# A quarter of q in fp32 by SyncE, z ahead of kv in the opening, and a reordered batch 1 and chunk 1

## The chip, the cores and the metric

The kernel runs on one core of a Trainium2 chip. The metric is the device time of one execution in microseconds (us). The core has a matmul engine (TensorE, PE; PEld is its weight load), a vector engine (VectorE, DVE), a scalar engine for pointwise functions (ScalarE, ACT), a general engine (GpSimd, POOL) and a sequencer without arithmetic (SyncE, SP). SP, ACT and POOL can issue transfers (DMAs). An engine executes its own instructions in program order; between engines the order comes from semaphores. Matmul results land in PSUM, eight banks of 512 fp32 columns on 128 partitions; everything else lies in SBUF.

## The reference

The inputs are q, k and v, each (8 batches, 8 heads, 576 positions, 64), and two weights, w_in (512 x 2048) and w_out (2048 x 512), all fp32.

```
def phi(x):
    return np.where(x > 0, x, np.exp(x) - 1.0) + 1.0
q_p, k_p = (phi(q), phi(k))
kv = np.einsum('bhsd,bhse->bhde', k_p, v)
z = np.sum(k_p, axis=2)
num = np.einsum('bhsd,bhde->bhse', q_p, kv)
den = np.einsum('bhsd,bhd->bhs', q_p, z)[..., None] + 1e-06
x = (num / den), heads side by side: 4608 rows of 512
h = x @ w_in
out = (h - np.tanh(h)) @ w_out
```

phi is computed as min(exp(x), max(x, 0) + 1), with an exp on ScalarE, a maximum with an addition on VectorE (`r`), and a minimum on VectorE.

## The kernel before

**Two stages.** The attention works batch by batch (576 rows each) and writes xT, the normalised result transposed to 512 x 4608 in bf16. The two dense layers work in nine chunks of 512 rows. Layer 1 of a chunk computes 16 groups `fi` of 128 hidden columns (four 512-column matmuls each, L366), two groups at a time go through tanh (L372, in chunk 0 one at a time, L377) and a subtraction into gT (L373, L378). Layer 2 runs in 16 steps `s` of four matmuls (L387); a finished row block is copied out of PSUM by ScalarE (`evac`, L396) and stored by two transfers of SP (L401). In chunk 0 layer 2 is cut the other way round: step s works with the weights of quarter `s // 4` on row block `s % 4`, so that it starts with a quarter of w_out, and all four evacuations come in steps 12 to 15. Layer 1 and the later chunks' layer 2 rotate over PSUM banks 0 to 5; attention work uses banks 6 and 7, in chunk 0 banks 4 to 7 (`side`).

**Order by hand.** The program order is the schedule. The lists `s1[fi]` and `s2[s]` hold attention work that is issued after group fi of layer 1 and after step s of layer 2. In chunk c the work of batch c + 1 (`n1`) is finished and that of batch c + 2 (`n2`) is begun. The work of a batch is: load q, k, v (POOL transfers that cast fp32 to bf16; a tile holds rows in two halves i, each half in two parts h), phi of k and q (`a_kphi`, `a_qphi`, L134 to L136), the transposes of q (`a_qT_pe` on TensorE, L164 with copies at L168 and L170, or a transposing transfer of SP, `a_qT_dma`, L153), kv and z by matmuls over the positions with a mask product into kz (`a_kv`, L177 and L186; or `a_kv_cols`, L199 and L202, which reads a copy `vp` of v with a column of ones behind it, made by `a_vp`, L189), the denominators (`a_den`, L276, L281, reciprocal L285), and the numerators. The reciprocals reach all partitions through DRAM (`a_spread`: four stores of SP into ds, L305, two broadcast loads into rdb, L308; `a_num` then multiplies, L317 and L328), or, for batches 0 and 1, by a matmul with a selection matrix (`b0_spread`, L240; `a_spread_pe`, L354, after `a_split`, L295 to L298, has cut the reciprocal into bf16 parts), with the numerators copied to `ns` by ScalarE first (L233; L344 and L346) and multiplied at L244 and L359.

**The loads.** POOL issues, in this order: q(0) in two halves, k(0) in two halves, the identity matrix, v(0) in two halves, w_in in ten parts, k(1), two quarters of w_out, q(1), some memsets, v(1), two quarters of w_out. Eight of POOL's transfers can be out at once: the ninth waits for the first, and so on. From chunk 1 on, POOL waits at `gate` (L383) for the transposed q of batch c + 1 before it issues the loads of batch c + 2.

**The opening.** Up to the first dense layer the order is: phi of q(0), half by half; 18 matmuls on zeros (`spin`, L444); transposes of half 0; phi of k(0) half 0, exp of k(0) half 1 in two parts; five spins; transposes of half 1; a selection matrix built on ScalarE (L460, L462); six spins; z of half 0 (`b0_z`, L210); the minima of k half 1; z's mask product (`b0_zc`, L214); kv of half 0 (`b0_kv`, L221) and its mask product (`b0_kz`, L225); z of half 1 and its mask product; the denominators of batch 0; numerators, kv of half 1, spread and scaling (L231 to L244). `b0_scale_rest` (L263) finishes the last 64 rows of batch 0 in chunk 0.

**Chunk 0 and chunk 1.** In chunk 0, `s2[7]` holds both halves of the transposes of q(1) and then kv of batch 1, `s2[8]` the rest of batch 0, `s2[9]` the denominators of batch 1, `s2[10]` its numerators and the split, `s2[11]` and `s2[13]` the two halves of the spreading; phi of q(2) lies in `s2[12]` to `s2[14]` (the last with the transposing transfer), phi of k(2) half 0 in `s2[15]`. In chunk 1, `s1[1]` has phi of k(2) half 1, `s1[3]` the two copies of v(2), `s1[7]` kv of batch 2 and `s1[10]` its denominators and their spreading; its numerators are in `s2[11]` to `s2[15]`. From chunk 2 on kv is in `s1[5]` and the denominators in `s1[8]`.

The tile gT has one buffer, so each chunk's gT waits until the one before is read.

Of the kernel before, what the change touches and what calls it, by code (L numbers as in the profile page):

```python
# [18 lines left out]
def kernel(  # L19
# [9 lines left out]
    nc = tc.nc  # L29
# [55 lines left out]
    def load(b, t, src, halves):  # L85

        x = src[b].rearrange("h (p j) d -> (h p) (j d)", j=J)
        if halves:
            for i in range(2):
                nc.gpsimd.dma_start(out=t[:, :, i].rearrange("q h j d -> q h (j d)"),  # L90
                                    in_=x.rearrange("(h i q) x -> i q h x", h=2, i=2)[i])
        else:
            nc.gpsimd.dma_start(out=t.rearrange("q h i j d -> q (h i) (j d)"),
                                in_=x.rearrange("(n q) x -> q n x", n=4))
# [26 lines left out]
    def phi_pieces(b, src, store, name, i, parts=0):  # L121

        if i == 0:
            store[b] = work.tile([128, 2, J, 2, D], BF16, name=name)
        x = src[b][:, :, i]
        e = epool.tile([128, 2, J, D], BF16, name="e")
        r = epool.tile([128, 2, J, D], BF16, name="r")
        y = store[b][:, i].rearrange("p j h d -> p h j d")
        if parts:

            return ([lambda h=h: nc.scalar.activation(e[:, h], x[:, h], AF.Exp) for h in range(2)],
                    lambda: nc.vector.tensor_scalar(r, x, 0.0, 1.0, ALU.max, ALU.add),
                    [lambda h=h: nc.vector.tensor_tensor(y[:, h], e[:, h], r[:, h], ALU.min) for h in range(2)])
        return (lambda: nc.scalar.activation(e, x, AF.Exp),  # L134
                lambda: nc.vector.tensor_scalar(r, x, 0.0, 1.0, ALU.max, ALU.add),  # L135
                lambda: nc.vector.tensor_tensor(y, e, r, ALU.min))  # L136
# [54 lines left out]
    def a_kv_cols(b, banks):  # L191
        kp = kp_t[b]
        kz_t[b] = kz_c[b % 2]
        ps = [banks()[:, 0:272].rearrange("p (i e) -> p i e", i=2) for hg in range(2)]
        for i in range(2):
            for j in range(J):
                for hg in range(2):
                    r = slice(64 * hg, 64 * hg + 64)
                    nc.tensor.matmul(ps[hg][:, i, :], kp[r, i, j].rearrange("p h d -> p (h d)"),  # L199
                                     vp[r, i, j, :], start=(j == 0), stop=(j == J - 1))  # L200
        for hg in range(2):
# [205 lines left out]
    nc.scalar.activation(act0, zero[:, 0:1], AF.Exp)  # L407
    load_q(0)
# [44 lines left out]
    (ek0, rk0, mk0), (ek1, rk1, mk1) = (phi_pieces(0, k_t, kp_t, "kp", i, 2 * i) for i in range(2))  # L453
    for f in (ek0, rk0, *ek1, mk0, rk1):
        f()
# [46 lines left out]
    for c in range(NC):  # L502
# [4 lines left out]
        if c == 0:  # L507
# [35 lines left out]
            s2[12].append(lambda: q2(0))  # L543
            s2[13].append(lambda: (spread1(1), q2(1)))
            s2[14].append(lambda: q2(2))
            s2[15].append(lambda: a_kphi(2, 0))
        elif n1 < B:
            s1[7 if c == 1 else 5].append(lambda: a_kv_cols(n1, attn))
            s1[10 if c == 1 else 8].append(lambda: (a_den(n1, attn), a_spread(n1)))
            for p in range(NP + 1):  # L550
                s2[(11 if c == 1 else 9) + p].append(lambda p=p: a_num(n1, p))
        if c == 1:
            s1[1].append(lambda: a_kphi(2, 1))
            for i in range(2):
                s1[3].append(lambda i=i: a_vp(2, i))
# [87 lines left out]
```

## Time and profile before

| | value |
|---|---|
| runs | median 295.15 us of 4 (294.8 to 295.48) |
| profiled execution | 295.1 us, of which the span from the first to the last instruction is 293.3 |
| granted TensorE clock | 0.998 |
| first exp of q(0) (L134) | 5.70 us |
| reciprocal of batch 0 (L285) | 13.71 to 14.77 us |
| steady L366 from | 17.77 us |
| layer 2 of chunk 0 (L387) from | 31.16 us |
| layer 1 of chunk 1 (L366) from | 51.22 us |
| layer 1 of chunk 2 (L366) from | 82.34 us |
| end of the last L387 group on the chain of waits | 279.18 us |
| q0, POOL's transfers | 18.35 MB in 17,552 packets |
| q1, transfers of SP | 20.17 MB in 21,344 packets |

A profile row gives start and duration in us, engine and line, the operation with output<-input, the shape and how many instructions are merged; a bracket holds the idle time in front of it and what ended it. Lines are those of the kernel before. A matmul's duration is longer than the distance to the next one, because matmuls are pipelined. Durations of a transfer are either the issuing time on its queue (rows of SPq and POOL) or the time to landing, where the row says so. Idle time of an engine that is not on the path to the end costs nothing by itself.

### The profile page before, as it was taken

The page shows a single profiled execution, that of the slowest core. Times are in us where ns is not written, and L with a number is a line of the kernel's source. Part 1 is how long each engine was busy: PE and PEld are TensorE (multiplying, and loading weights), DVE is VectorE, ACT ScalarE, POOL GpSimd, SP SyncE. Part 2 cuts the span into 40 slices and gives each one's busy share as a digit, 9 for nine tenths or more (in the row PEclk, how much of TensorE's full clock was granted, in tenths as well). Part 3 has the DMA queues.
Part 4 walks back from the last instruction along what each step waited for, and adds up shares of the span by engine and source line. Part 5 has one row for each costly group of instructions (what it writes and reads, how often), then busy time and mean ns, then how long its engine had stood idle before and what let it go on. Part 6 is the DMA issues. An engine that isn't in the chain of part 4 may idle for free.

```text
span 293.3 us, 4475 instructions
## 1 busy us (share of the span) xinstructions
PE 283.7 (97%) x1772; PEld 134.3 (46%) x1801; DVE 174.7 (60%) x265; ACT 139.5 (48%) x168; POOL 33.5 (11%) x55
## 2 busy tenths in 40 slices
PE   8899998999999999999999999999999999999994
PEld 2544453354444444544454445444444444444443
DVE  4759957887467764786478646865581456106600
ACT  3938537947334653455246524661452155126411
POOL 8673030030030003000300020000000000000000
PEclk9999999999999999999999999999999999999999
DMA  7999999987999658955895669577117310131032
GB/s 99 194 204 213 208 206 217 205 141 139 239 161 194 153 122 139 220 126 117 137 223 127 141 134 179 114 176 146 38 25 176 73 36 0 38 81 27 0 74 72
DMA packets 39077, 38.94 MB, mean 133 GB/s; under 512 B 16336, under 2 KB 33808, under 8 KB 38288
## 3 DMA queue, kind: packets, MB, share of 16 engines
q0 software_dynamic: 17552, 18.35, 38.8%
q1 hardware_dynamic: 21344, 20.17, 30.1%
q8 instruction: 14, 0.23, 0.3%
q10 hardware_dynamic: 160, 0.13, 0.1%
q14 instruction: 7, 0.06, 0.1%
HBM read 43.91 MB, written 9.55 MB: 182 GB/s over the span
## 4 chain that ended last, share of the span: by engine, by line
PE 69%; DMA 17%; issue 7%; POOL 2%; DVE 1%; ACT 1%; SPq 1%; POOLq 0%; DVEq 0%
PE ps_all L366 34%; PE ps_all L387 30%; DMA qraw<-in_q_dram 6%; DMA w_in_sb<-in_moe_w_in_dram 3%; DMA rdb<-ds 3%; PE ps_all L199 2%; DMA out_dram<-osb 2%; DMA kraw<-in_k_dram 2%; PE ps_all L317 2%; DMA ds<-rden 1%; PE ps_all L276 1%; ACT osb L396 1%; SPq L401 0%; POOL qraw L90 0%; ACT e L134 0%
## 5 line engine op out<-in xcount | busy, mean ns | idle before, releaser
L366 PE MATMUL ps_all<-xT,w_in_sb 128*128 128x512 bf16 x560 | 127.0, 379 | 1.1 <-DVE xT L244 0.3
L387 PE MATMUL ps_all<-w_out_sb,gT 128*128 128x512 bf16 x547 | 126.3, 379 | 0.7
L373 DVE TENSOR_TENSOR gT<-ps_all,th 128x1024 bf16<-128x1024 f32 x64 | 77.9, 1218 | 59.8 <-ACT th L372 59.8
L372 ACT ACTIVATE th<-ps_all 128x1024 f32<-128x1024 f32 x64 | 65.5, 1024 | 57.0 <-PE ps_all L366 46.4
L366 PEld LDWEIGHTS <-w_in_sb 128*128 128x128 bf16 x576 | 55.2, 98 | 66.6 <-issue 0.6
L387 PEld LDWEIGHTS <-gT 128*128 128x128 bf16 x560 | 54.1, 98 | 64.5 <-issue 0.6
L396 ACT COPY osb<-ps_all 128x512 f32<-128x512 f32 (+1 forms) x36 | 20.9, 582 | 73.7 <-PE ps_all L387 57.4
L328 DVE TENSOR_TENSOR xT<-ps_all,rdb 128x512 bf16<-128x512 f32 x24 | 16.3, 689 | 13.7 <-PE ps_all L317 11.2
L134 ACT ACTIVATE e<-qraw 128x1152 bf16<-128x1152 bf16 x16 | 18.5, 1161 | 7.0 <-DMA qraw<-in_q_dram 7.0
L134 ACT ACTIVATE e<-kraw 128x1152 bf16<-128x1152 bf16 x15 | 17.5, 1165 | 0.1
L136 DVE TENSOR_TENSOR qp<-e,r 128x1152 bf16<-128x1152 bf16 x16 | 12.0, 757 | 8.0 <-ACT e L134 7.4
L136 DVE TENSOR_TENSOR kp<-e,r 128x1152 bf16<-128x1152 bf16 x15 | 11.4, 758 | 8.1 <-ACT e L134 7.3
L383 POOL COPY g<-qT 1x1 bf16<-1x1 bf16 x5 | 1.1, 226 | 120.9 <-DMA qT<-qp 120.9
L378 DVE TENSOR_TENSOR gT<-ps_all,th 128x512 bf16<-128x512 f32 x16 | 10.3, 685 | 2.4 <-ACT th L377 1.7
L377 ACT ACTIVATE th<-ps_all 128x512 f32<-128x512 f32 x16 | 9.2, 598 | 4.3 <-PE ps_all L366 3.1
L317 PE MATMUL ps_all<-qT,kz 128*128 128x512 bf16 x28 | 10.1, 379 | 0.2 <-DVE xT L328 0.2
L444 PE MATMUL ps_all<-zero 128*128 128x512 bf16 x29 | 8.8, 464 | 1.2 <-DVE zero L405 1.2
L135 DVE TENSOR_SCALAR r<-qraw 128x1152 bf16<-128x1152 bf16 x16 | 7.3, 454 | 2.2 <-DMA qraw<-in_q_dram 2.2
L199 PE MATMUL ps_all<-vp,kp 64*128 64x136 bf16 x216 | 7.4, 220 | 0.4 <-POOL g L383 0.4
L199 PEld LDWEIGHTS <-kp 64*128 64x128 bf16 x216 | 6.4, 94 | 3.0 <-issue 2.1
L285 DVE RECIPROCAL rden<-den 128x144 f32<-128x144 f32 x7 | 7.4, 1053 | 0.2
L394 DVE COPY osb<-ps_all 128x128 f32<-128x128 f32 x1 | 0.3, 291 | 11.6 <-DMA out_dram<-osb 11.6
(82 smaller groups left out, 121.8 us busy)
## 6 DMA issues: line engine op xcount, KB each, us to landing
out_dram<-osb SPq DMA_DIRECT2D x70, 128.0 KB
rdb<-ds SPq DMA_DIRECT2D x12, 576.0 KB
kraw<-in_k_dram POOLq DMA_DIRECT2D x7, 576.0 KB, 7.4
qraw<-in_q_dram POOLq DMA_DIRECT2D x7, 576.0 KB, 9.0
v<-in_v_dram POOLq DMA_DIRECT2D x7, 576.0 KB, 11.9
w_out_sb<-in_moe_w_out_dram POOLq DMA_DIRECT2D x4, 512.0 KB, 16.2
w_in_sb<-in_moe_w_in_dram POOLq DMA_DIRECT2D x6, 256.0 KB, 8.7
qraw<-in_q_dram POOLq DMA_DIRECT2D x2, 288.0 KB, 4.8
```

Source lines behind the costliest of these rows:

```text
L134: return (lambda: nc.scalar.activation(e, x, AF.Exp), lambda: nc.vector.tensor_scalar(r, x, 0.0, 1.0, ALU.max, ALU.add), lambda: nc.vector ...
L136: lambda: nc.vector.tensor_tensor(y, e, r, ALU.min))
L199: nc.tensor.matmul(ps[hg][:, i, :], kp[r, i, j].rearrange("p h d -> p (h d)"), vp[r, i, j, :], start=(j == 0), stop=(j == J - 1))
L317: nc.tensor.matmul(ps, kz[:, p // 2, p % 2, 0:128], qT[:, p % 2, 0:8, p // 2, :], start=True, stop=True)
L328: nc.vector.tensor_mul(xT[:, p, S * b:S * b + 512].rearrange("p (j t c) -> p j t c", j=8, t=4), ps.rearrange("p j (t c) -> p j t c", t=4), ...
L366: nc.tensor.matmul(h, w_in_sb[:, 2 * (p % 2) + p // 2, fi * 128:(fi + 1) * 128], xT[:, p, c * 512:(c + 1) * 512], start=(n == 0), stop=(n ...
L372: nc.scalar.activation(th, h, AF.Tanh)
L373: nc.vector.tensor_sub(gT[:, fi:fi + 2, :], h, th)
L377: nc.scalar.activation(th, h, AF.Tanh)
L378: nc.vector.tensor_sub(gT[:, fi, :], h, th)
L387: nc.tensor.matmul(o, gT[:, fi, i * 128:(i + 1) * 128], w_out_sb[:, fi, :], start=(fi == 0), stop=(fi == NF - 1))
L396: nc.scalar.copy(osb[:, f0:f1], o[:, f0:f1])
```

## The change

In the opening, half 0 of q(0) comes by two transfers instead of one: SP loads its part h = 0 as fp32 into `q_f`, a tile that takes the buffer of gT and is viewed as fp32, and POOL loads part h = 1 as bf16. Half 1 of k(0) comes by two POOL transfers, one for each part. `phi_pieces` gets a list `xs` of the two parts in place of the flag `parts`, and then gives exp, maximum and minimum part by part. It is used for half 0 of q(0) and for half 1 of k(0). The spins are 14, 5 and 5 in place of 18, 5 and 6. z of both halves with their mask products stands ahead of kv of half 0.

In chunk 0, kv of batch 1 stands between the two halves of the transposes; denominators, numerators and split of batch 1 are together in `s2[9]`; phi of q(2) is one step later (13, 14, 15), and its transposing transfer is now issued in step 15, after that step's evacuation and stores.

In chunk 1, the copies of v(2) are made by ScalarE (`a_vp_act`) in `s1[3]` and `s1[5]`; the exp of k(2) half 1 is in `s1[1]` and its maximum and minimum in `s1[3]`; kv of batch 2 is cut into half 0 in `s1[8]` and half 1 with the mask products in `s1[9]`; the denominators and their spreading are in `s1[11]`. Numerators stay where they are.

```diff
 def load(b, t, src, halves):
             for i in range(2):
+                if t is k_t.get(0) and i == 1:
+
+                    for h in range(2):
+                        nc.gpsimd.dma_start(out=t[:, h, i].rearrange("q j d -> q (j d)"),
+                                            in_=x.rearrange("(h i q) x -> h i q x", h=2, i=2)[h, i])
+                    continue
+                if t is q_t.get(0) and i == 0:
+
+                    nc.sync.dma_start(out=q_f, in_=x.rearrange("(h i q) x -> h i q x", h=2, i=2)[0, 0])
+                    nc.gpsimd.dma_start(out=t[:, 1, i].rearrange("q j d -> q (j d)"),
+                                        in_=x.rearrange("(h i q) x -> h i q x", h=2, i=2)[1, 0])
+                    continue
...
-    def phi_pieces(b, src, store, name, i, parts=0):
+    def phi_pieces(b, src, store, name, i, xs=None):
...
-        if parts:
-
-            return ([lambda h=h: nc.scalar.activation(e[:, h], x[:, h], AF.Exp) for h in range(2)],
-                    lambda: nc.vector.tensor_scalar(r, x, 0.0, 1.0, ALU.max, ALU.add),
+        if xs:
+
+            return ([lambda h=h: nc.scalar.activation(e[:, h], xs[h], AF.Exp) for h in range(2)],
+                    [lambda h=h: nc.vector.tensor_scalar(r[:, h], xs[h], 0.0, 1.0, ALU.max, ALU.add)
+                     for h in range(2)],
                     [lambda h=h: nc.vector.tensor_tensor(y[:, h], e[:, h], r[:, h], ALU.min) for h in range(2)])
...
+    def a_vp_act(b, i):
+        nc.scalar.copy(vp[:, i, :, 0:128].rearrange("p j (h d) -> p h j d", h=2), v_b[b % 2][:, 0:2, i])
+
-    def a_kv_cols(b, banks):
+    def a_kv_cols(b, banks, i_s=(0, 1), ps=None):
...
-        for i in range(2):
+        for i in i_s:
...
+        if i_s == (0,):
+            return ps
...
+    q_f = gpool.tile([128, NF, 512], BF16, name="gT").rearrange("p a b -> p (a b)").bitcast(F32)[:, 0:J * D]
     load_q(0)
...
-    (eq0, rq0, mq0), (eq1, rq1, mq1) = (phi_pieces(0, q_t, qp_t, "qp", i) for i in range(2))
-    for f in (eq0, rq0, mq0, eq1, rq1, mq1):
+    q_h = [q_f.rearrange("p (j d) -> p j d", d=D), q_t[0][:, 1, 0]]
+    eq0, rq0, mq0 = phi_pieces(0, q_t, qp_t, "qp", 0, q_h)
+    eq1, rq1, mq1 = phi_pieces(0, q_t, qp_t, "qp", 1)
+    for f in (eq0[0], rq0[0], eq0[1], rq0[1], *mq0, eq1, rq1, mq1):
         f()
-    spin(18)
+    spin(14)
     a_qT_pe(0, 0, side, "AV")
...
+    ek1, rk1, mk1 = phi_pieces(0, k_t, kp_t, "kp", 1, [k_t[0][:, h, 1] for h in range(2)])
+    for f in (ek0, rk0, *ek1, mk0):
         f()
     spin(5)
...
-    spin(6)
+    spin(5)
     b0_z(0)
-    for f in mk1:
-        f()
+    for h in range(2):
+        rk1[h]()
+        mk1[h]()
     b0_zc(0)
+    b0_z(1)
+    b0_zc(1)
     b0_kv(0)
     b0_kz(0)
-    b0_z(1)
-    b0_zc(1)
     a_den(0, Banks([4]))
...
-            s2[7].append(lambda: (a_qT_pe(1, 0, side), a_qT_pe(1, 1, side), a_kv(1, side)))
+            s2[7].append(lambda: (a_qT_pe(1, 0, side), a_kv(1, side), a_qT_pe(1, 1, side)))
             s2[8].append(lambda: b0_scale_rest(side))
-            s2[9].append(lambda: a_den(1, side))
-            s2[10].append(lambda: (num1(), a_split(1)))
+            s2[9].append(lambda: (a_den(1, side), num1(), a_split(1)))
...
-            s2[12].append(lambda: q2(0))
-            s2[13].append(lambda: (spread1(1), q2(1)))
-            s2[14].append(lambda: q2(2))
-            s2[15].append(lambda: a_kphi(2, 0))
+            s2[13].append(lambda: (spread1(1), q2(0)))
+            s2[14].append(lambda: q2(1))
+            s2[15].append(lambda: (q2(2), a_kphi(2, 0)))
         elif n1 < B:
-            s1[7 if c == 1 else 5].append(lambda: a_kv_cols(n1, attn))
-            s1[10 if c == 1 else 8].append(lambda: (a_den(n1, attn), a_spread(n1)))
+            if c == 1:
+                s1[8].append(lambda: sub.update(kv=a_kv_cols(n1, attn, (0,))))
+                s1[9].append(lambda: a_kv_cols(n1, attn, (1,), sub["kv"]))
+            else:
+                s1[5].append(lambda: a_kv_cols(n1, attn))
+            s1[11 if c == 1 else 8].append(lambda: (a_den(n1, attn), a_spread(n1)))
...
         if c == 1:
-            s1[1].append(lambda: a_kphi(2, 1))
-            for i in range(2):
-                s1[3].append(lambda i=i: a_vp(2, i))
+            k21 = phi_pieces(2, k_t, kp_t, "kp", 1)
+            s1[1].append(k21[0])
+            s1[3].append(lambda: (k21[1](), k21[2](), a_vp_act(2, 0)))
+            s1[5].append(lambda: a_vp_act(2, 1))
```

More of the change, by code (lines that the diff above doesn't have):

```diff
@@ L189, in a_vp @@
         nc.vector.tensor_copy(vp[:, i, :, 0:128].rearrange("p j (h d) -> p h j d", h=2), v_b[b % 2][:, 0:2, i])
-    def a_kv_cols(b, banks):
+    def a_vp_act(b, i):
+        nc.scalar.copy(vp[:, i, :, 0:128].rearrange("p j (h d) -> p h j d", h=2), v_b[b % 2][:, 0:2, i])
+    def a_kv_cols(b, banks, i_s=(0, 1), ps=None):
         kp = kp_t[b]
         kz_t[b] = kz_c[b % 2]
-        ps = [banks()[:, 0:272].rearrange("p (i e) -> p i e", i=2) for hg in range(2)]
-        for i in range(2):
+        ps = ps or [banks()[:, 0:272].rearrange("p (i e) -> p i e", i=2) for hg in range(2)]
+        for i in i_s:
             for j in range(J):
@@ L447 @@
     kz_t[0] = kz_c[0]
-    (eq0, rq0, mq0), (eq1, rq1, mq1) = (phi_pieces(0, q_t, qp_t, "qp", i) for i in range(2))
-    for f in (eq0, rq0, mq0, eq1, rq1, mq1):
+    q_h = [q_f.rearrange("p (j d) -> p j d", d=D), q_t[0][:, 1, 0]]
+    eq0, rq0, mq0 = phi_pieces(0, q_t, qp_t, "qp", 0, q_h)
+    eq1, rq1, mq1 = phi_pieces(0, q_t, qp_t, "qp", 1)
+    for f in (eq0[0], rq0[0], eq0[1], rq0[1], *mq0, eq1, rq1, mq1):
         f()
-    spin(18)
+    spin(14)
     a_qT_pe(0, 0, side, "AV")
-    (ek0, rk0, mk0), (ek1, rk1, mk1) = (phi_pieces(0, k_t, kp_t, "kp", i, 2 * i) for i in range(2))
-    for f in (ek0, rk0, *ek1, mk0, rk1):
+    ek0, rk0, mk0 = phi_pieces(0, k_t, kp_t, "kp", 0)
+    ek1, rk1, mk1 = phi_pieces(0, k_t, kp_t, "kp", 1, [k_t[0][:, h, 1] for h in range(2)])
+    for f in (ek0, rk0, *ek1, mk0):
         f()
```

## The prediction

> **What bounds the kernel.** I read the page's busy shares first, then TensorE's timeline for holes, then what ends each hole, and last the DMA share by stage.
>
> ```profile
> PE 283.7 (97%) x1772; PEld 134.3 (46%) x1801; DVE 174.7 (60%) x265; ACT 139.5 (48%) x168; POOL 33.5 (11%) x55
> ```
>
> ```profile
> 17.77 13.55 PE L366 MATMUL ps_all<-xT,w_in_sb 128*128 128x512 bf16 x61
> ...
> 39.09 0.68 PE L164 MATMUL ps_all<-ident,qp 128*128 128x128 bf16 x9 [0.36 <-DVE qp L136]
> 39.70 1.66 PE L177 MATMUL ps_all<-v,kp 64*128 64x192 bf16 x36
> 41.30 1.03 PE L387 MATMUL ps_all<-w_out_sb,gT 128*128 128x512 bf16 x3
> ...
> 47.18 0.31 PE L354 MATMUL ps_all<-w,sel 32*128 32x144 bf16 x8 [0.69 <-ACT ns L344]
> ...
> 58.66 1.24 PE L199 MATMUL ps_all<-vp,kp 64*128 64x136 bf16 x36 [0.37 <-POOL g L383]
> ...
> 80.07 0.38 PE L317 MATMUL ps_all<-qT,kz 128*128 128x512 bf16 x1 [0.16 <-DVE xT L328]
> ```
>
> Read the start times. From 17.77 us TensorE issues a 512-column matmul every 0.216 us (steps in the timeline), and the time is that work plus the opening, four holes and a tail after 279 us that the change does not touch. Start to start, the holes are 0.52 us at 39.09, 0.85 at 47.18 (previous matmul 46.11 + 0.216), 0.53 at 58.66 (57.91 + 0.216) and 0.33 at 80.07 (79.52 + 0.216). The modelled ends make the bracketed idle a little shorter. After 80 us no hole above 0.1 us is left, so whatever the third L317 group gains at 80.07 the whole kernel gains.
>
> The DMA queue hides a second bound. Columns: window, its length, PE busy (count), clock, DMA share, GB/s.
>
> ```profile
> 0.00:2.50 2.50, 1.31 (x4) 1.00 0.00 0
> 2.50:3.50 1.00, 1.00 (x4) 1.00 0.72 37
> 3.50:5.00 1.50, 1.50 (x5) 1.00 1.11 182
> 5.00:41.00 36.00, 33.92 (x310) 1.00 1.24 203
> ```
>
> ```profile
> L115 POOL DMA_DIRECT2D w_out_sb<-in_moe_w_out_dram x1: 762/762/762, 23.3 to 23.3; - x1
> ...
> DMA to landing us min/median/max: 18.0/18.0/18.0
> ```
>
> The engines move nothing until 2.5 us and are then full to beyond 41 us. The third part of w_out, issued at 23.25, lands at 41.25; the L387 row at 41.30 is the first that reads it. So until 41.3 us the kernel is tied to the POOL queue's bytes, with TensorE only 0.1 us behind.
>
> **Part 1, the opening.** A quarter of q leaves POOL's queue for SP's. Written as bf16 it is 147 KB, 0.73 us at 203 GB/s: the most by which everything behind it (q's other half, k, v, all weights, batch 1) can come forward. Call the gain D. SP is free from 0.65 us. Its nearest rows are a 128 KB store in an idle stage (issue 279.81, landed 282.68: 2.9 us) and the small ds writes under load (4.0 us), so the quarter lands between 3.6 and 4.9 us. It runs mostly in the empty stretch before 2.5 us and the 37 GB/s microsecond after it, with some overlap with POOL's first packets. Bounds of D: 0 if it only interleaves, 0.73 if it fills idle time; it is nearest to the second, and I take **0.6**.
>
> Against this stands the Trainium skill, "DMA: Bandwidth & Descriptors", section "Issuing engines are not separate DMA queues": transfers from any issuer share the same 16 engines, so a second issuer saves only issue time. By that sentence D would be 0 and the time the slower rival's below; the empty 2.5 us is why I do not follow it here.
>
> The other opening edits. POOL issues five loads for four, so identity and v go out 0.7 us later (one issue, L90, 0.73): v's first part is issued near 5.5, but its packets only follow k's, which land near 9.9 (10.50 - 0.6), so the backlog covers it. The halved exps add 0.2 us of ScalarE (two of 0.68 for one of 1.16), the halved maxima and minima some 0.3 of VectorE. The exp and the maximum on the fp32 part have no row; the maximum lies between 0.23 (half of 0.45) and 0.69 (an fp32 product of 128x512), and both run while POOL's quarter is awaited. The first transposes come near 6.3 instead of 7.71: POOL's own quarter lands near 5.1 (5.70 - 0.6), its exp ends at 5.8, its minimum at 6.25; four fewer spins of 0.43 (timeline steps before 5.4) keep TensorE free for them. k's second half starts its exps at the first quarter (near 9.6, before 10.59), its minima end near 11.75 instead of 12.33, z(1), kv(0), the 16 denominator matmuls and the mask follow, and the reciprocal starts near 13.1 instead of 13.71. With z(1) ahead of kv(0) the 0.4 us of z(1) no longer stand behind v's landing (12.02). Dense L366 then starts at about 17.1 (17.77 - 0.7). The borrowed gT buffer costs nothing: its readers end before 6.3, and gT is first written at 20.98.
>
> **Part 2, chunk 0's second layer.** kv(1) between the transposes fills the 0.52 hole. But TensorE, then 0.7 + 0.5 = 1.2 us early, meets v(1) (landed 22.52 + 16.2 = 38.7, less D) and w_out's third part (41.25, less D): L387 starts at 40.7, and only D of the 1.2 survives. **Gain here 0.6**, not 1.2. The two masks of kv (0.89) and the second transposes' copies (0.69 on ScalarE, 0.42 on VectorE) lie under the eight L387 matmuls (1.9 with the small ones) ahead of L276, which reads them. The numerators of batch 1 are issued one step of four matmuls (0.86) earlier, so the ns copies (44.80 to 47.13) end 0.8 earlier. Next in line is the split reciprocal on VectorE:
>
> ```profile
> 46.10 0.37 DVE L298 SCALAR_TENSOR_TENSOR w<-t,part,u 128x144 bf16<-128x144 bf16 x1
> ```
>
> It ends at 46.47 when TensorE arrives at 46.33, so 0.15 to 0.2 stays: **gain 0.7** (0.4 to 0.85). Chunk 1 starts at 51.22 - 1.3 = 49.9.
>
> **Part 3, chunk 1's first layer**, on the clock of before. Rows that decide:
>
> ```profile
> 55.53 2.10 ACT L372 ACTIVATE th<-ps_all 128x1024 f32<-128x1024 f32 x2
> ...
> 58.16 0.82 DVE L189 COPY vp<-v 128x1152 bf16<-128x1152 bf16 x2
> ...
> 61.16 0.78 DVE L202 TENSOR_TENSOR kz<-ps_all,mask 128x272 bf16<-128x272 f32 x2
> ...
> 64.30 1.05 DVE L285 RECIPROCAL rden<-den 128x144 f32<-128x144 f32 x1
> ```
>
> VectorE loses 0.82 us of copies, ScalarE gains two. No ScalarE copy of this shape is in the trace; the nearest is the 128x1152 exp, 1.16 (lower bound 0.8 from the 0.67 of 128x640, upper 1.5). q(2)'s exps move one step back, so ScalarE runs: first tanh 54.0 (was 53.58), exp of k(2), second tanh 56.0, copy 56.9, third tanh 58.0, copy 58.9, fourth 60.0, fifth 60.9. kv no longer waits 0.53, since its halves come after the 9th and 10th groups. But the fifth subtraction and the two kz follow on VectorE: 62.2 to 63.4, kz to 64.1. The denominator matmul now stands two groups of four after kv instead of three, and TensorE reaches it at 62.95: a **new wait of 1.2** (0.85 even with ScalarE on time, by chunk 2's rows: kz ends 3.2 after the group ahead of kv, TensorE needs 2.3), and 0.2 for banks. Behind it in order stand all of L366. TensorE loses 1.4 - 0.53 = **0.9** (0.3 to 1.1). The reciprocal comes behind the sixth subtraction and ends at 66.7 instead of 65.35: **1.4 later** (1.3 with ScalarE on time, 1.8 with copies of 1.5).
>
> **Part 4, what the reciprocal feeds.**
>
> ```profile
> 79.32 1.89 DVE L328 TENSOR_TENSOR xT<-ps_all,rdb 128x512 bf16<-128x512 f32 x3 [2.55 <-DMA rdb<-ds]
> ```
>
> rdb, twice through DRAM, releases xT, and xT the third numerator at 80.07, which is 14.7 us after the reciprocal. After: 65.35 - 1.3 + 1.4 + 14.7 = 80.15. TensorE itself would be there at 79.74 - 1.3 + 0.9 = 79.35 and waits. One thing eases it: qT(2)'s transpose, now behind the last store on SP's queue, is issued near 52.9 (before 53.40), so POOL's gate opens and batch 3's loads, among which the ds writes run, end up to 0.5 earlier. I take half, 0.25: 79.9 against 80.07.
>
> **Sum:** -0.6 - 0.7 + 1.4 - 0.25 = -0.15, say -0.2. The profiled run took 295.1 (span 293.3 and 1.8 around it; the median of the runs is 295.15): **294.9**.
>
> **Rivals.** (1) *Forecast*: the gains of the first 50 us are eaten by the later reciprocal; 294.9, its own range 294.6 to 295.6. Chance 0.45; 0.2% is 0.59 us, about what a measurement tells from no change. (2) *Faster*: the quarter fills idle time fully (0.73), the hole at 47.18 closes (0.85), the reciprocal is only 1.3 late and the ds writes gain the whole 0.5: -0.73 - 0.85 + 1.3 - 0.5 = -0.8, **294.3**; if the order on VectorE lets the reciprocal come 0.5 sooner than I sum, 293.8. For it: DMA at 0 until 2.5 us. Against: the wait for kz stands in chunk 2's rows. Chance 0.34. (3) *Slower*: the fp32 quarter interleaves and w_out's third part lands no earlier than 41.25. Its place is L387 at 41.30; D = 0 leaves -0.7 + 1.4 = +0.7, **295.8**, and it decides from D below 0.1. For it: 37 GB/s at 2.5 us is first-packet latency which SP's queue pays too. Chance 0.21. (4) *The opening does not get shorter* because SP's first transfer is late: up to 4.9 us nothing changes, as q's second half (7.24 - 0.6) is the next wait; it is part of the forecast.
>
> The three give faster 0.34, same 0.45, slower 0.21, and a range of **294.0 to 295.9** with about 0.1 left out on each side.
>
> **What would show it.** Right: DMA busy before 2.5 us; w_out's third part landed near 40.65 with L387 on it; the hole at L354 under 0.3; L276 of chunk 1 waiting about 1 us for kz L202; the third L317 waiting for rdb longer than the 0.33 of before. Wrong: no wait at L276, or rdb landed more than 0.6 away from 79.0, or w_out's third part landed at 41.2 again.

## The result, and the profile after

| | median of the runs | ratio to before, 95% interval |
|---|---|---|
| before | 295.10 us (52 runs, 294.55 to 296.46) | |
| after | 295.88 us (32 runs, 294.95 to 297.6) | 1.0028 [1.002, 1.0036] |

The changed kernel is 0.28% slower. Its profiled execution took 297.13 us (span 295.4) and is one of its four slowest, all with a mean granted clock of 0.994 or less; an execution at full clock, of a kernel with the same order and eleven more spins, comes with the experiments (e_spin). The page's row of busy time has barely moved:

```profile
PE 283.8 (96%) x1767; PEld 134.2 (45%) x1796; DVE 175.1 (59%) x266; ACT 141.6 (48%) x171; POOL 33.5 (11%) x56
```

TensorE does the same 284 us of work, so what was added is waiting. The stages of the opening (window, length, then busy time and count of PE, PEld, DVE, ACT and POOL, the clock, DMA share, GB/s):

```profile
0.00:2.50 2.50, 1.31 (x4) 0.49 (x5) 1.35 (x8) 1.49 (x2) 1.46 (x6) 1.00 0.27 74
2.50:3.50 1.00, 1.00 (x4) 0.40 (x3) 0.82 (x12) 0.00 (x0) 1.00 (x3) 1.00 0.90 156
...
5.00:14.00 9.00, 5.43 (x86) 3.00 (x84) 5.59 (x14) 6.70 (x13) 5.73 (x10) 1.00 1.18 179
14.00:18.00 4.00, 4.00 (x63) 2.43 (x58) 1.91 (x3) 1.39 (x2) 3.32 (x5) 0.57 1.31 203
```

The row of 5 to 14 us before:

```profile
5.00:14.00 9.00, 8.05 (x115) 4.32 (x113) 6.00 (x14) 7.42 (x13) 6.22 (x10) 1.00 1.22 190
```

In the first 2.5 us, idle before, the engines now move 74 GB/s, as meant. But from 5 to 14 us they move 179 GB/s where they moved 190, TensorE is busy 5.4 of 9 us instead of 8.05 (a part of that is the spins left out), and behind that the clock falls to 0.57. The third part of w_out, by the rows of its issue:

```profile
L127 POOL DMA_DIRECT2D w_out_sb<-in_moe_w_out_dram x1: 762/762/762, 23.5 to 23.5; - x1
...
DMA to landing us min/median/max: 18.0/18.0/18.0
```

Issued at 23.52 it lands at 41.5, not at 40.65; before it was 41.25. TensorE's timeline (start, duration, engine, line, operation):

```profile
43.02 1.03 PE L405 MATMUL ps_all<-w_out_sb,gT 128*128 128x512 bf16 x3
...
48.24 0.30 PE L372 MATMUL ps_all<-w,sel 32*128 32x144 bf16 x8
...
52.28 0.59 PE L384 MATMUL ps_all<-xT,w_in_sb 128*128 128x512 bf16 x2
...
64.74 0.72 PE L294 MATMUL ps_all<-qT,kz 128*32 128x144 bf16 x16 [0.31 <-DVE kz L220]
...
82.07 0.38 PE L335 MATMUL ps_all<-qT,kz 128*128 128x512 bf16 x1 [0.54 <-DVE xT L346]
```

These are the rows of before at 41.30 (L387), 47.18 (L354), 51.22, 62.53 (L276) and 80.07 (L317). Dense L384 is steady from 20.02 instead of 17.77 (+2.25), chunk 1 starts +1.06 late, so chunk 0 made up 1.2; the third L335 group is +2.00 late, and so is the end (297.13 against 295.1). Two holes of chunk 0 are gone, a new wait for kz is there, and the wait for rdb has grown.

### The profile page after: what moved, and what is told of

Its sections match the earlier page's. It is cut to its first block, busy times and chain, and to the rows that moved or that the text cites. A ratio compares the mean times of both kernels' runs of the same rounds, so it can differ in the third digit from the quotient of the medians.

```text
span 295.4 us, 4467 instructions
## 1 busy us (share of the span) xinstructions
PE 283.8 (96%) x1767; PEld 134.2 (45%) x1796; DVE 175.1 (59%) x266; ACT 141.6 (48%) x171; POOL 33.5 (11%) x56
## 4 chain that ended last, share of the span: by engine, by line
PE 85%; DMA 7%; DVE 3%; ACT 2%; issue 1%; SPq 1%; POOL 0%; DVEq 0%; ACTq 0%; POOLq 0%
PE ps_all L384 39%; PE ps_all L405 37%; DMA rdb<-ds 3%; PE ps_all L215 2%; DMA kraw<-in_k_dram 2%; PE ps_all L335 2%; DMA ds<-rden 1%; DVE gT L396 1%; PE ps_all L294 1%; DMA out_dram<-osb 1%; PE ps_all L258 1%; ACT th L395 1%; PE ps_all L190 1%; PE ps_all L239 1%; DVE xT L262 0%
## 5 line engine op out<-in xcount | busy, mean ns | idle before, releaser
L384 PE MATMUL ps_all<-xT,w_in_sb 128*128 128x512 bf16 x560 | 127.3, 379 | 1.1 <-DVE xT L262 0.3
L384 PEld LDWEIGHTS <-w_in_sb 128*128 128x128 bf16 x576 | 55.1, 98 | 66.7 <-issue 0.9
L147 ACT ACTIVATE e<-qraw 128x1152 bf16<-128x1152 bf16 x15 | 17.3, 1162 | 2.6 <-DMA qraw<-in_q_dram 2.6
L149 DVE TENSOR_TENSOR qp<-e,r 128x1152 bf16<-128x1152 bf16 x15 | 11.4, 758 | 7.1 <-ACT e L147 6.2
L335 PE MATMUL ps_all<-qT,kz 128*128 128x512 bf16 x28 | 10.1, 379 | 0.5 <-DVE xT L346 0.5
L464 PE MATMUL ps_all<-zero 128*128 128x512 bf16 x24 | 7.1, 448 | 1.2 <-DVE zero L423 1.2
L148 DVE TENSOR_SCALAR r<-qraw 128x1152 bf16<-128x1152 bf16 x15 | 6.7, 454 | 0.9 <-DMA qraw<-in_q_dram 0.9
```

The source lines that it names most:

```text
L147: return (lambda: nc.scalar.activation(e, x, AF.Exp), lambda: nc.vector.tensor_scalar(r, x, 0.0, 1.0, ALU.max, ALU.add), lambda: nc.vector ...
L335: nc.tensor.matmul(ps, kz[:, p // 2, p % 2, 0:128], qT[:, p % 2, 0:8, p // 2, :], start=True, stop=True)
L384: nc.tensor.matmul(h, w_in_sb[:, 2 * (p % 2) + p // 2, fi * 128:(fi + 1) * 128], xT[:, p, c * 512:(c + 1) * 512], start=(n == 0), stop=(n ...
```

## The experiments

Two theories at first. **Reciprocal**: chunk 1's late denominators delay rdb and eat what was gained. **Late loads**: the quarter makes POOL's loads land later; in later expectations it is called **skew**, with some of the 16 DMA engines left behind by another amount in each execution. The first four profiles brought a third, **transpose**: what times rdb is the transposing transfer of q(2) on SP's queue, through POOL's gate and batch 3's loads. And the clock records a fourth, **clock**: too little TensorE work in the opening halves the clock in some executions.

Ratios are to the kernel before, run beside each; 0.001 is 0.3 us. Each kernel has one profile, of one execution, which can lie far from the median of its runs: e_noM3's took 1.4 us less, e_noCkv's 1.3 more. A reading of one profile is therefore weaker than a difference of runs.

| run | what is changed | median | ratio [95%] |
|---|---|---|---|
| e_O | opening only | 295.92 | 1.0038 [1.0025, 1.0052] |
| e_Q | SP's quarter only | 295.04 | 1.0016 [1.0004, 1.0027] |
| e_M | chunk 0 only | 294.92 | 1.0000 [0.9991, 1.0008] |
| e_M3 | phi of q(2) a step later only | 295.52 | 1.0014 [1.0006, 1.0023] |
| e_M12 | chunk 0 without that step | 294.28 | 0.9972 [0.9961, 0.9983] |
| e_M12z | e_M12, opening without quarter | 294.12 | 0.9981 [0.9967, 0.9996] |
| e_M12O | e_M12, whole opening, more spins | 294.55 | 0.9989 [0.9978, 1.0000] |
| e_C | chunk 1 only | 295.76 | 1.0034 [1.0021, 1.0047] |
| e_Ckv | its kv and denominators only | 295.90 | 1.0038 [1.0025, 1.0052] |
| e_Cvp | its copies by ScalarE only | 295.28 | 1.0016 [1.0007, 1.0025] |
| e_noC | all but chunk 1 | 295.46 | 1.0033 [1.0018, 1.0048] |
| e_noM3 | all but phi of q(2) | 295.47 | 1.0013 [0.9997, 1.0029] |
| e_noQ | all but the quarter | 295.57 | 1.0018 [1.0009, 1.0026] |
| e_noCkv | all but kv and denominators | 295.51 | 1.0022 [1.0008, 1.0037] |
| e_spin | all, more spins | 296.20 | 1.0039 [1.0027, 1.0051] |
| e_again | all, once more | 297.06 | 1.0069 [1.0043, 1.0095] |

### The parts: e_noC, e_C, e_O, e_M

The diff of each is a part of the change. e_noC puts back the chunk 1 of before, e_C has only chunk 1, e_O only the opening, e_M only this:

```diff
-            s2[7].append(lambda: (a_qT_pe(1, 0, side), a_qT_pe(1, 1, side), a_kv(1, side)))
+            s2[7].append(lambda: (a_qT_pe(1, 0, side), a_kv(1, side), a_qT_pe(1, 1, side)))
...
-            s2[9].append(lambda: a_den(1, side))
-            s2[10].append(lambda: (num1(), a_split(1)))
+            s2[9].append(lambda: (a_den(1, side), num1(), a_split(1)))
...
-            s2[12].append(lambda: q2(0))
-            s2[13].append(lambda: (spread1(1), q2(1)))
-            s2[14].append(lambda: q2(2))
-            s2[15].append(lambda: a_kphi(2, 0))
+            s2[13].append(lambda: (spread1(1), q2(0)))
+            s2[14].append(lambda: q2(1))
+            s2[15].append(lambda: (q2(2), a_kphi(2, 0)))
```

> The changed kernel with chunk 1 as it was before (opening and chunk 0 changed only). Reciprocal theory: the changed chunk 1 makes batch 2's reciprocal 1.4 to 1.6 us late against the chunk's start, and through rdb the third L317 group with it; without it the time is 295.9 - 1.5 = 294.4 us, chunk 1 has no wait in front of its denominators and the reciprocal follows the start of chunk 1 by 13.1 us as before. Late-load theory: the slowest DMA engines make the opening late and chunk 1 costs nothing; then it stays at 295.7 to 296.0 us. The prediction's own sum without part 3 would be 295.1 - 0.6 - 0.7 - 0.25 = 293.6.

> The kernel before with only chunk 1 changed. Reciprocal theory: chunk 1 starts at 51.2 us as before, the reciprocal comes 1.4 to 1.6 us later, the third L317 group stands at 81.5 to 81.7 instead of 80.07, and the time is 296.5 to 296.7 us. Late-load theory: the loads are those of before, so the time stays at 295.1 us. The prediction's terms give 295.1 + 1.4 = 296.5.

> The kernel before with only the opening changed. Prediction (D = 0.6): dense L384 at 17.1 us, third part of w_out landed near 40.65, 294.5 us. Late-load theory (D = -0.3 as in the profile of the changed kernel): the third part of w_out lands at 41.5 to 41.6, the opening is late by 0.3 to 1, and the time is 295.4 us or more. Clock theory: the granted clock falls to a half in the opening in some runs and not in others; then the runs lie in two groups some 1.3 us apart, the mean clock of the slow group below 0.996. Reciprocal theory says nothing of it.

> The kernel before with only chunk 0's second layer changed. Prediction: the hole at 39.09 closes, but the third part of w_out lands at 41.25 and takes the gain back; the hole in front of the spreading matmul shrinks from 0.85 to 0.15, chunk 1 starts at 50.5 instead of 51.22, and the third L317 group at 79.4: 294.4 us. Late-load theory agrees with it, since the loads are untouched. If the chain of rdb is bound by something other than the reciprocal (the loads on the queue), the gain of 0.7 is lost again: 295.1.

Opening and chunk 1 each cost 1.0 to 1.1 us alone. e_O fits the late-load theory and is 1.4 above the prediction; e_C lies between the two theories. The costs do not add up: without chunk 1's part (e_noC) the time stays within the interval of the whole change, which the reciprocal theory did not expect. (Four of e_noC's twelve runs had a fallen clock; without them its mean is still 0.55 above before.) And e_M gains nothing although its hole in front of L359 shrank from 0.85 to 0.20. TensorE's timeline of e_M shows a part of where the gain went. This execution is the slowest of e_M's eleven, and in it the third part of w_out landed at 41.92, 0.7 later than before:

```profile
59.03 1.18 PE L202 MATMUL ps_all<-vp,kp 64*128 64x136 bf16 x34 [0.75 <-DVE vp L189]
```

Before, this wait of kv(2) was 0.37. The exps of q(2), a step later, hold back ScalarE's first tanhs of chunk 1 and with them VectorE's copies of v. The second cost is on SP's queue, in the next runs.

### The late transfer: e_M3, e_M12, e_noM3

e_M3 is the kernel before with only the last seven lines of the diff above; e_M12 is e_M without them; e_noM3 is the changed kernel without them.

> The kernel before with only phi of q(2) and its transposing transfer one step later. Transpose theory: the transfer is issued behind all eight stores, 0.85 later (54.25 instead of 53.40), and the third L317 group stands 0.6 to 0.85 later: 295.5 to 295.8 us. Reciprocal theory: the reciprocal of batch 2 is only as late as ScalarE's first tanh of chunk 1 (0.4 at most), 295.1 to 295.3 us. The prediction gave this move no cost of its own.

> The kernel before with kv of batch 1 between its transposes and denominators, numerators and split of batch 1 together in s2[9], but phi of q(2) and its transposing transfer at their old steps. Transpose theory (new, from the profiles so far: the third L317 group follows the issue of the transposing transfer of q(2) on SP's queue by 26.2 to 26.8 us in every kernel, whenever the reciprocal comes): the transfer is issued 0.65 earlier, near 52.75, the third L317 group stands at 79.4, and the time is 294.2 to 294.5 us, faster than before by 0.1 to 0.2%. Reciprocal theory says the same here, since the reciprocal too comes 0.65 earlier. If the late step of phi of q(2) is not what took the gain in the run of chunk 0 alone, this stays at that run's 294.9 us.

> The changed kernel with phi of q(2) and its transposing transfer at the steps of before; the opening, the rest of chunk 0 and chunk 1 changed. Transpose theory: the transfer goes out 0.85 earlier, the third L317 group comes 0.5 to 0.85 earlier and the time falls from 295.9 to 295.1-295.4 us. Reciprocal theory: chunk 1's late reciprocal decides and stays, 295.7 to 295.9 us.

SP's queue in the kernel before, in e_M3 and in e_M12 (start, issue time, line):

```profile
53.40 2.65 SPq L153 DMA_TRANSPOSE qT<-qp  x1
...
65.38 1.29 SPq L305 DMA_DIRECT2D ds<-rden  x4
70.77 1.12 SPq L308 DMA_DIRECT2D rdb<-ds  x2
```

```profile
54.28 2.88 SPq L153 DMA_TRANSPOSE qT<-qp  x1
65.78 1.28 SPq L310 DMA_DIRECT2D ds<-rden  x4
71.38 1.12 SPq L313 DMA_DIRECT2D rdb<-ds  x2
```

```profile
52.50 2.54 SPq L153 DMA_TRANSPOSE qT<-qp  x1
...
64.48 1.29 SPq L310 DMA_DIRECT2D ds<-rden  x4
69.74 1.12 SPq L313 DMA_DIRECT2D rdb<-ds  x2
```

The rdb loads wait for the ds writes, whose landing the trace does not give; rdb's issue stands for it. They land about when batch 3's loads end: v(3) lands at 70.5, 71.2 and 69.8 (issue plus time to landing), rdb is issued at 70.77, 71.38 and 69.74. In all eighteen profiles rdb's issue lies between 0.5 us ahead of v(3)'s landing and 0.7 behind it. The loads start when the gate's copy has run, 4.8 us after the transposing transfer in all three kernels (58.22, 59.08, 57.29). So the transfer, which in e_M3 goes behind two more stores and the last evacuation, times the third numerator in these three. e_M3's 295.52 and e_M12's 294.28 lie where the transpose theory had them (the reciprocal theory had the same for e_M12, and 295.1 to 295.3 for e_M3); e_M12 and e_M12z are the fastest of all and beat both kernels. What is left in its chunk 0 is the wait that the prediction named:

```profile
41.06 1.02 PE L392 MATMUL ps_all<-w_out_sb,gT 128*128 128x512 bf16 x4 [0.25 <-DMA w_out_sb<-in_moe_w_out_dram]
```

e_noM3's median, 0.41 us below that of the whole change, lies just above what the transpose theory had, and its interval overlaps that of the whole change, with runs from 293.97 to 296.51.

### Chunk 1 in pieces: e_Ckv, e_Cvp, e_noCkv

```diff
-            s1[7 if c == 1 else 5].append(lambda: a_kv_cols(n1, attn))
-            s1[10 if c == 1 else 8].append(lambda: (a_den(n1, attn), a_spread(n1)))
+            if c == 1:
+                s1[8].append(lambda: sub.update(kv=a_kv_cols(n1, attn, (0,))))
+                s1[9].append(lambda: a_kv_cols(n1, attn, (1,), sub["kv"]))
+            else:
+                s1[5].append(lambda: a_kv_cols(n1, attn))
+            s1[11 if c == 1 else 8].append(lambda: (a_den(n1, attn), a_spread(n1)))
```

e_Ckv is the kernel before with this, e_Cvp with the other lines of chunk 1; e_noCkv is the changed kernel without this.

> The kernel before with kv of batch 2 cut into s1[8] and s1[9] and its denominators in s1[11], the copies of v(2) still on VectorE in s1[3]. If the chain transpose - gate - batch 3's loads - rdb decides alone: 295.0 us, since the gate opens as before. If a late reciprocal costs a part of its delay (its denominators stand one group of 0.86 us later, so some 0.5 to 0.9 later): 295.2 to 295.5 us.

> The kernel before with the copies of v(2) on ScalarE and the maximum and minimum of k(2)'s second half in s1[3]; kv and denominators of batch 2 at their old steps s1[7] and s1[10]. ScalarE's two copies of 1.18 each delay its tanhs; kv then waits for the second copy (ending near 59.0 plus 1) longer than the 0.53 of before, TensorE loses 0.9 to 1.6 in chunk 1 and the reciprocal as much: 295.6 to 296.4 us by the prediction's way of counting; 295.0 to 295.2 us if the gate alone decides.

> The changed kernel with kv of batch 2 in one piece in s1[7] and its denominators in s1[10] as before; the copies of v(2) stay on ScalarE, and the opening and chunk 0 stay changed. Reciprocal theory (half of the reciprocal's delay reaches rdb; alone these steps cost 1.1 us and ScalarE's copies 0.45): the time falls by 0.3 to 0.6 us, to 295.2-295.6. Transpose theory alone: the transfer's place is unchanged, so the time stays at 295.9.

e_Ckv alone costs more than was expected. Its TensorE and SP rows, from the slowest of its five runs:

```profile
63.97 0.72 PE L281 MATMUL ps_all<-qT,kz 128*32 128x144 bf16 x16 [0.25 <-DVE kz L207]
...
81.44 0.38 PE L322 MATMUL ps_all<-qT,kz 128*128 128x512 bf16 x1 [0.68 <-DVE xT L333]
```

```profile
53.73 2.71 SPq L153 DMA_TRANSPOSE qT<-qp  x1
...
67.37 1.29 SPq L310 DMA_DIRECT2D ds<-rden  x4
72.19 1.12 SPq L313 DMA_DIRECT2D rdb<-ds  x2
```

The transfer is 0.33 late (this execution was 0.3 behind before the changed part began), the ds writes 2.0 and rdb 1.4. Here v(3) lands at 71.5 and the ds writes 0.7 behind it. So the gate is not all: in this execution the late reciprocal puts the ds writes behind the loads. e_C, which has the same order and ScalarE's copies besides, does not show it: its profile is the fastest of its runs (295.05, with chunk 1 starting 0.25 early), its reciprocal is 1.5 later against the start of chunk 1 than before, and yet rdb is issued at 70.89 and the third numerator stands at 79.94 (before 70.77 and 80.07). What e_C's other runs pay, 295.32 to 296.16, has no profile. In e_Cvp the copies by ScalarE hold up kv in its middle. TensorE itself comes later by it: the third numerator then stands at 80.20 without a wait in front of it.

```profile
59.65 0.71 PE L202 MATMUL ps_all<-vp,kp 64*128 64x136 bf16 x18 [0.71 <-ACT vp L192]
```

Both theories seem right in part. From the profiles:

| | L1 of chunk 1 | transfer | reciprocal | rdb issued | third numerator |
|---|---|---|---|---|---|
| before | 51.22 | 53.40 | 64.30 | 70.77 | 80.07 |
| e_M12 | 50.32 | 52.50 | 63.39 | 69.74 | 78.99 |
| e_M3 | 51.24 | 54.28 | 64.69 | 71.38 | 80.40 |
| e_noM3 | 50.12 | 52.31 | 64.70 | 69.87 | 79.07 |
| e_C | 50.97 | 53.16 | 65.56 | 70.89 | 79.94 |
| e_Ckv | 51.54 | 53.73 | 66.28 | 72.19 | 81.44 |
| e_spin | 50.60 | 53.64 | 65.31 | 71.58 | 80.81 |
| after | 52.28 | 55.32 | 66.99 | 72.97 | 82.07 |

In the eighteen profiles a straight line through the gate's opening and the ds writes gives rdb within 0.45 us, with a weight of 0.55 for the gate and 0.5 for the ds writes. That is a fit, and in most kernels the two move together. e_noM3 and e_C show that a late reciprocal is mostly hidden if the transfer is early; e_Ckv that it is not always. e_noCkv's median lies where the reciprocal theory had it, but it falls by less than its interval is wide; it does not decide between the two.

### The quarter: e_Q, e_noQ, e_M12z

e_Q is the kernel before with the quarter, its phi pieces and 14 spins; e_noQ is the changed kernel without this, and so with 18 spins; e_M12z is e_M12 with k in two loads and z ahead of kv:

```diff
+                if t is q_t.get(0) and i == 0:
+                    nc.sync.dma_start(out=q_f, in_=x.rearrange("(h i q) x -> h i q x", h=2, i=2)[0, 0])
```

> The kernel before with only the quarter of q in fp32 on SP's queue (and the phi pieces and 14 spins that go with it); k's loads and the order of z and kv as before. Skew theory: the SP transfer leaves some of the 16 DMA engines behind, by another amount in each execution, so the loads' last pieces land anywhere between 0.4 earlier and 1 later; the median is 0.4 to 0.8 us above before (295.3 to 295.7) and the runs scatter over more than 1.3 us, where those of before lie within 1. Prediction (D = 0.6): 294.5 us. If the cost of the opening lies in z and k and not in the quarter: 294.9 us with a narrow scatter.

> The changed kernel with half 0 of q(0) by one POOL transfer as before (no SP transfer; 18 spins), everything else changed. Late-load theory: the loads land as in the kernel before, the third part of w_out near 41.2 instead of 41.5, and the time is 0.3 to 0.6 us below the changed kernel: 295.3 to 295.6 us. If the rest of the opening is what costs (z ahead of kv, k in two loads), it stays at 295.9 us. Prediction (D = 0.6): without the quarter it is 0.6 slower than the changed kernel, 296.4 us. Clock theory: with 18 spins no run has a mean clock below 0.996.

> The fastest version so far (chunk 0's kv between the transposes, denominators and numerators together, phi of q(2) at its old steps) with the rest of the opening added: k's second half in two loads and z ahead of kv, but no quarter on SP. Prediction's terms for these: kv(0) no longer waits behind z(1)'s 0.4 us and the exps of k's second half start at its first quarter, so up to 0.4 faster than 294.3: 293.9 us. Skew theory: no quarter, so a narrow scatter, and whatever the opening gains is held up again at the third part of w_out, so 294.2 to 294.4. If z and k are what costs in the opening: 294.7 us or more.

e_Q costs 0.16%, some 0.5 us (its median is 0.2 above that of before beside it), and scatters over 1.8 us (294.54 to 296.38; 1.2 without its one run with a fallen clock), e_noQ over 0.9. e_Q's median lies between the prediction's and the skew theory's; e_noQ's lies where the late-load theory had it. Among the runs with a mean clock above 0.994 the standard deviation is 0.43 to 0.78 us in the eight kernels with the quarter and 0.18 to 0.49 in the eight changed ones without it. The trace has the moment at which each of the 16 engines is done with a load. For the second half of v(0):

```
            first   last   spread
before      12.69   13.36   0.67
e_C         12.68   13.27   0.59
e_M12z      12.43   13.41   0.98
e_Q         12.04   13.48   1.44
e_O         12.52   14.10   1.58
after       12.11   13.94   1.83
```

With the quarter the fastest engine of these rows is up to 0.65 us early and the slowest up to 0.74 late, and a load is there when the slowest is. The spread is 1.19 to 1.83 us in all nine profiles with the quarter and 0.48 to 1.06 in the nine without it. Over these two sets, the reciprocal of batch 0 starts at 14.40 and 13.73 on average (eight of the nine have the other edits of the opening too), and the third part of w_out lands at 41.4 (40.8 to 42.3) and 41.3 (41.0 to 41.9). Late loads is right, but as a scatter: e_noM3's profile, with an early set, took 294.08 us.

The spread is not the whole of it. The average of the 16 engines is done with the third part of w_out at 40.13 with the quarter and at 40.20 without, the slowest at 41.41 and 41.27. So the spread takes 0.2 us of the 0.6 that were expected, and the rest is missing on the average engine too. What the queues had moved (MB):

| | POOL's queue by 5 us | SP's quarter, fp32 | POOL's queue from 5 to 9 us |
|---|---|---|---|
| before | 0.31 | - | 0.73 |
| after | 0.29 | 0.29 | 0.63 |
| e_spin | 0.22 | 0.29 | 0.73 |

The quarter stands for 0.147 MB that POOL need not write. With it, the changed kernel is 0.12 MB ahead at 5 us, which is the expected 0.6 us, and loses it by 9 us, where POOL's queue is slower; in e_spin the lead is small from the start. On average of the nine profiles the lead is 0.10 MB at 5 us and nothing at 9 us. What slows POOL's queue there no run shows.

e_M12z shows that z and k cost nothing measurable, nor bring anything beyond e_M12.

### The clock: e_spin, e_M12O, e_again

```diff
-    spin(14)
+    spin(18)
...
-    spin(5)
+    spin(12)
     b0_z(0)
```

> The changed kernel with 18, 5 and 12 spins instead of 14, 5 and 5. Clock theory: with TensorE kept busier before 14 us no execution has a mean clock below 0.996; the slow tail above 297 goes, and the median falls by 0.1 to 0.3 us to 295.6-295.8. If the tail is the DMA's alone, it stays, with runs above 296.4 in one of six. If spins stand in the way of the transposes or of z, the median rises by up to 0.4.

> The fastest version (chunk 0's kv between the transposes, denominators and numerators together, phi of q(2) at its old steps, chunk 1 as before) with the whole changed opening, the quarter of q on SP among it, and 18, 5 and 12 spins. Skew theory: the quarter makes the landings of the loads scatter, so the median is 0.3 to 0.8 above 294.2 and the scatter over 1.3 us. Clock theory: with these spins it is the clock that scattered the opening, and this lies within 0.3 of 294.2, with a narrow scatter. Prediction (D = 0.6): 293.6 us.

> The changed kernel once more, for a profile of an execution in which the granted clock does not fall in the opening. Expected 295.4 to 296.2 us, mean clock 0.997 or more, dense L384 from 17.5 to 18.5 rather than 20.02. What both theories then say of chunk 1: by the transpose theory the transposing transfer of q(2) is issued 3.04 after layer 1 of chunk 1 starts (before 2.18); by the reciprocal theory the reciprocal starts 14.7 after it (before 13.1); the third L317 group waits for rdb by 0.5 or more.

Windows of the changed kernel and of e_spin (columns as above):

```profile
10.80:14.20 3.40, 1.77 (x64) 1.15 (x66) 2.49 (x8) 3.33 (x10) 1.69 (x3) 1.00 1.31 198
14.20:17.60 3.40, 3.40 (x56) 2.14 (x48) 1.89 (x3) 1.19 (x2) 2.94 (x5) 0.51 1.32 205
```

```profile
10.80:14.20 3.40, 2.96 (x80) 1.74 (x79) 2.55 (x8) 3.17 (x9) 1.66 (x4) 1.00 1.31 194
14.20:17.60 3.40, 2.82 (x43) 1.48 (x40) 2.81 (x5) 1.83 (x2) 2.96 (x5) 1.00 1.30 202
```

Of 77 runs of kernels with 14, 5 and 5 spins and the quarter, 15 have a mean clock of 0.994 or less, and all but one of these are above 296.3; of the 24 runs with 18, 5 and 12 spins none has. (Of e_M12z's nine, with 18, 5 and 5 spins and no quarter, one has.) So this part of the clock theory holds: the clock makes the tail. It does not make the median: without its runs with a fallen clock the changed kernel's mean is 295.78, still 0.7 above before. e_spin's median did not fall but rose by 0.3, as was expected if spins stand in the way of the transposes or of z; which of them does was not tried. e_again, meant as a profile at full clock, had a fallen clock in both its runs; what was expected of its chunk 1 came all the same (transfer 3.04 and reciprocal 14.7 behind its start). e_M12O is some 0.5 us above e_M12, with intervals that just overlap; that is the cost of the whole opening with more spins, not of the quarter alone.

e_spin's profile is the changed order at full clock, in TensorE's and SP's rows:

```profile
50.60 8.07 PE L384 MATMUL ps_all<-xT,w_in_sb 128*128 128x512 bf16 x35
...
63.05 0.72 PE L294 MATMUL ps_all<-qT,kz 128*32 128x144 bf16 x16 [0.31 <-DVE kz L220]
...
80.81 0.38 PE L335 MATMUL ps_all<-qT,kz 128*128 128x512 bf16 x1 [0.95 <-DVE xT L346]
```

```profile
53.64 2.95 SPq L166 DMA_TRANSPOSE qT<-qp  x1
66.40 1.29 SPq L323 DMA_DIRECT2D ds<-rden  x4
71.58 1.12 SPq L326 DMA_DIRECT2D rdb<-ds  x2
```

Chunk 1 starts 0.62 us earlier than before. But the transfer goes out 3.04 us behind that start instead of 2.18, so 0.24 later than before, and the ds writes 1.0 later. TensorE stands idle 0.95 for rdb, the third numerator is 0.74 late, and the execution takes 295.8, 0.7 more than that of before.

## Why the prediction was wrong

The forecast was 294.9 us, no change; measured is the number of its slower rival (295.8 forecast, 295.88 measured). One half of that rival's condition held: the third part of w_out landed no earlier. The other did not, since the quarter went through the idle stretch. The step that failed is **D = 0.6** of part 1, the gain of the queue by the quarter: the profiles show about 0 in its place, and the runs no gain (e_Q, the quarter alone, +0.16%). In its own terms, with e_spin for the measured side:

| term | forecast | measured |
|---|---|---|
| D at the third part of w_out | -0.6 | about 0 (+0.15 on average of nine profiles) |
| hole in front of the spreading matmul | -0.7 | -0.65 (1.071 to 0.418 start to start) |
| reciprocal against the start of chunk 1 | +1.4 | +1.63 |
| loads ending earlier | -0.25 | transfer 0.24 later, not 0.5 earlier; -0.27 is what is left between the other terms, +1.01, and the third numerator, +0.74 |

With D at 0 and 1.63 for 1.4 the same sum gives +0.7: 295.8. That it closes is partly luck. The last term is wrong in its cause and right in size, because rdb follows the reciprocal only in part. And e_spin's profile took 295.8, where the median of its runs is 296.2.

- *The quarter fills idle time.* It did at first: 74 GB/s before 2.5 us and landed by 3.58 in the changed kernel, POOL's quarter's exp at 5.08 in e_spin (5.1 forecast). The inference from there was wrong: the lead at 5 us, 0.5 us on average of the nine profiles, was gone by 9 us, and the slowest of the 16 engines, for which a load waits, took 0.2 more. Why the lead goes stays open. The sentence of the Trainium skill that was set against it ("DMA: Bandwidth & Descriptors", "Issuing engines are not separate DMA queues": a second issuer saves issue time only) came out right in size, D near 0, though the quarter itself did come earlier.
- *Dense work 0.7 earlier, reciprocal at 13.1.* In e_spin the reciprocal starts at 14.27 and steady dense work at 18.33, 0.56 later than before. Besides the loads, k's second half has its last minimum at 12.84 (11.75 forecast), where its halved maxima and minima alternate on VectorE.
- *Part 2* was right: the hole of 0.52 filled, its gain taken back by w_out (e_M12's row at 41.06), the hole at L354 worth 0.65. Its cost elsewhere was only half seen: part 4 had the transfer behind the last store, 3.0 us after the start of chunk 1, but counted it as an easing, because the start of chunk 1 was forecast 1.3 early; alone this step costs 0.4 us (e_M3). The hold-up of ScalarE's tanhs was priced in chunk 1.
- *Part 3*: the wait for kz was forecast as 1.2 and is 0.47 start to start; the reciprocal's delay was near.
- *Part 4*: "14.7 us after the reciprocal" is not the rule. The third numerator follows the reciprocal's end by 14.7 us before, 14.4 in e_spin and 13.3 in e_noM3 and e_C; by the fit rdb follows the gate and the ds writes, about half each.
- *Its signs*: the DMA was busy before 2.5 us, and the hole in front of the spreading matmul is 0.2 in e_spin. Two signs of being wrong came: w_out's third part landed at 41.03 in e_spin and 41.5 in the changed kernel, and the product that waits for rdb starts at 80.06 in e_spin, 1 us behind the 79.0.
- *Not foreseen*: with four spins fewer and less work early on the clock falls in a fifth of the executions, which are 1.0 to 1.5 us longer on average than the others of the same kernel. The prediction gave the spins no cost.

## What to carry over

A transfer that is moved in a queue is costed by all that its landing opens: here a late transpose held a gate, the gate the next batch's loads, and these a small write, and a matmul some 27 us behind the transpose waited for it. When two chains meet in one wait, improving the rows ahead of it brings nothing until both are earlier; the gain of chunk 0's reordering (0.28%) came out only when its third edit was left out. And bytes moved to another queue are worth what the landings of later loads show, not the idle stretch that they fill: here the lead was there at 5 us and gone at 9 us.

## What was not expected of the hardware

- With a 288 KB load by SP ahead of POOL's loads, the spread of the 16 DMA engines at a later load (v(0), second half) is 1.2 to 1.8 us in nine profiles, against 0.5 to 1.1 in the nine without it, and it lasts: three loads further on it is 1.78 in the changed kernel (14.16 to 15.94) against 0.74 before (14.74 to 15.48).
- The clock fell to a half for one stretch of 3.41 us (14.26 to 17.67 in the changed kernel's profile) behind a stretch in which TensorE was busy 1.77 of 3.4 us, and stayed full behind one with 2.10 (e_noM3), 2.84 (before) or 2.96 (e_spin). The Trainium skill ("TensorE: Matmul & The Clock Gate", Part 1) gives a free-running window of that length and names idle windows as the cause; here a half-busy one was enough. Two other executions with 1.73 (e_O) and 1.79 (e_noC) in the same 3.4 us kept their clock. The position of the window explains a part of that. The stretches of the clock record are whole multiples of 3.41 us. On each record's own grid the last window ahead of the fall holds 1.78 (changed kernel), 1.65 (e_again) and 1.91 us (e_noCkv) of TensorE work; the emptiest windows of those that kept the clock hold 1.86 (e_noC), 2.02 (e_O) and 2.11 (e_noM3). So 1.86 was kept where 1.91 was not, and the busy time alone does not give the limit.
